# A fused attention and squared-ReLU kernel in which W_out's first blocks are stored earlier, its first further sums stand behind the norms, and the late conversions are placed differently

## The chip, the cores and the metric

The kernel runs on one core of one Trainium2 chip. The metric is device time in microseconds, the median of three runs. The profile is of one further execution with the hardware profiler on.

## What is computed

Linear attention without a softmax, a normalisation per head, and then a two-layer network with a squared ReLU, all in float32:

```python
kv = einsum('bhsd,bhse->bhde', k, v)            # 8 batches, 8 heads, 576 rows, 64 columns
out = einsum('bhsd,bhde->bhse', q, kv)
x = out / sqrt(mean(out * out, axis=-1) + 1e-6) * g_norm
x = x.transpose(0, 2, 1, 3).reshape(4608, 512)
h = x @ w_in                                    # w_in: 512 x 2048
g = maximum(h, 0) ** 2
return g @ w_out                                # w_out: 2048 x 512
```

The two weight matrices arrive as 64-bit floats, which the kernel reads as pairs of 32-bit words and converts itself.

## The kernel before

The 4608 rows are worked through in nine strips of 512 (index `s`). A strip first makes hidden values (the "up" steps), then multiplies them with W_out (the "down" steps). The products use Strassen-like schemes: seven products of blocks take the place of eight, and the sums of blocks that they need are made by VectorE, or by GpSimd, ahead of them. From strip 1 on the down products, and from strip 2 on the up products too, apply the scheme a second time, on 128 by 128 blocks.

Strip 0 is different, because the weights are still being loaded and converted while it runs. Its up steps are sixteen plain steps of `up_first` (4 column groups `g`, 2 halves `fh`, 2 parts `i`), its down steps are seven products `p` in the order 1, 2, 5, 6, 7, 3, 4, each in two halves, by `down`. `n_up` is the number of up steps, 16 here.

All instructions are recorded in program order, and each engine executes its own in that order (the pools are under `tc.manual_schedule()`). So the place of a call in the Python text sets the order of the work on each engine and on SyncE's (SP's) queue, from which nearly all DMAs are issued. In the compiled program the DMA issues take eight completion semaphores in turn, so that an issue also waits for the landing of the DMA eight issues before it.

The parts that matter here:

- `load` and `load_next` bring k, v and q of a batch and a pair of heads. `load_rest(b, eng)` brings the last 64 rows of k and of v for all heads of a batch `b` (`k_rest`, `v_rest`); for batch 0 it is called on ScalarE's queue, after all other first loads. `key_value` multiplies k and v, with the rest rows last, and ScalarE copies the product to `kv_all`.
- `load_piece` brings a raw piece of weights (128 x 512 words of 64 bits, 512 KB) into one of 8 buffers, `load_more` does so some pieces ahead. There are 32 pieces: 0 to 15 of W_in, 16 to 31 of W_out.
- `convert_on_act` makes two passes over a raw piece on ScalarE (`w_c`, and `raw` in place); `conversion` makes four on VectorE (L254 to L263). `convert_pieces` converts a pair of pieces and issues ScalarE's passes for the pair after it. `convert(n)` brings the list `conversions` up to entry `n`: 8 entries of `pieces_in`, 4 of `pieces_out`, 4 of `sums_out`.
- `pieces_out` converts half of W_out into places 4 and 5 of the tile `w_in`, which are free in strip 0. `sums_out` converts the other half into tiles `wt` (in the raw pool), makes the block W_out t1 in place 6 and four further blocks in `wt`, and stores these four in the DRAM tile `w_out`. The three blocks in places 4, 5 and 6 are called `w_first`; strip 0's products 1, 2 and 5 read them there. `down` stores each of them in `w_out` too, in two DMAs of 512 KB, in the step that follows its product. Later `sums_in` (called at down steps 7, 8, 9 and 12) scales W_in by g and overwrites places 4, 5 and 6 with sums of W_in's blocks.
- `deep_sums` makes four further sums of a W_out block on VectorE (`w_t`) and `store_deep_sums` stores them in the DRAM tile `w_deep`. `down` calls it in strip 0, in the first half of each product (in the second half for product 1). `stream` brings the block for a later product back from DRAM into `w_blk`; the tiles `w_t` and `w_blk` share one pool of four buffers, which takes over the memory of the raw pieces.
- `attend(n)` takes the next slices of the attention work: queries transposed (`t_ps`, `qT`), keys and values, products `x_ps`, their squares and means (`sq`, `ms`), roots, the normalised `x_n`, and its transpose `xt_ps` to `xT`. It is called after the products of each step.

The late conversions in strip 0's up steps are placed by these lines of the main loop:

```python
if 4 <= i < 11:
    convert(3 + i)          # ahead of the step's products
...
if 11 <= i < n_up:
    convert(5 + (3 * i + 2) // 4)   # behind the step's attention slices
```

Of the kernel before, what the change touches and what calls it, by code (L numbers as in the profile page):

```python
# [20 lines left out]
def kernel(  # L21
# [34 lines left out]
    nc = tc.nc  # L56
    P = 128
# [91 lines left out]
    def load_rest(b, eng):  # L149
        h = b % 2  # L150
        half = slice(REST * h, REST * (h + 1))
        for t, src in ((k_rest[half], k), (v_rest[half], v)):
            eng.dma_start(out=t, in_=src[b, :, C * P : S].rearrange("h s d -> s h d"))
# [20 lines left out]
    def load_next(q_eng=nc.sync, names="kvq"):  # L174
        u = next(to_load, None)
        if u is not None:
            load(*u, q_eng, names)
# [138 lines left out]
    conversions += [(pieces_out, j) for j in range(0, FQ, 2)] + [(sums_out, j) for j in range(0, FQ, 2)]  # L316
    converted = [NP // 2]

    def convert(n):
        while converted[0] < min(n, len(conversions)):  # L320
            fn, a = conversions[converted[0]]
            fn(a)
            converted[0] += 1
# [9 lines left out]
    nc.scalar.sqrt(one, one)  # L333

    load_next()
    for p in range(1, NP):
        load_next()
        load_piece()
# [2 lines left out]
    g_src = g_norm.rearrange("(d u) -> d u", u=1)  # L341
    for h in range(2):
        nc.scalar.dma_start(out=g_col[ts(h, D)], in_=g_src)
    load_rest(0, nc.scalar)


    qT, kvd, x_n, xt = {}, {}, {}, {}
# [476 lines left out]
    def store_deep_sums(p, w):  # L824
        if p == 6:

            parts = [sum_pool.tile([P, FQ // 2, P], FP32, name=f"w_t{i}", tag="sum") for i in range(4)]
            deep_sums(parts, w)
            for i, t in enumerate(parts):
                nc.sync.dma_start(out=w_deep[B_OUT[p], :, i], in_=t)  # L830
            return
        if p not in deep:
            reserve(p)
        t = deep.pop(p)
        deep_sums([t[:, i] for i in range(4)], w)
        nc.sync.dma_start(out=w_deep[B_OUT[p]], in_=t)

    def down(s, p, i):
        if i == 0:
            open_bank(p)  # L840
        a = {1: 11, 2: 21, 6: 11, 7: 12, 3: 21, 4: 22}.get(p)
        w = w_blk[s, p]
        product(
            p, i,
            lambda fc: (gq[s, 1, fc // 2][:, fc % 2] if p == 5 else gq[s, a][:, fc])[:, ts(i, P)],
            lambda fc: w[:, :, fc], FQ,
        )

        if i == (p == 1) and s == DEEP - 1:
            store_deep_sums(p, w)  # L850
        if i == 0:
            return
        del w_blk[s, p]

        if s == 0 and p in (2, 6, 3):
            reserve({2: 5, 6: 7, 3: 4}[p])
        if p not in (1, 7) and (s, p) not in ((0, 3), (0, 4)):
            stream()
        if s == 0 and p in (1, 2, 5):

            for e in range(2):
                nc.sync.dma_start(out=w_out[B_OUT[p], :, e], in_=w_first[B_OUT[p]][:, :, ts(e, P)])

        if p == (1 if s else 2):
            for g in range(NG):
                x = gq[s, 11][:, ts(g, 2)]
                minus(nc.vector, x, gq[s, 1, g], x)
        if p == (2 if s else 5):
            minus(nc.vector, gq[s, 21], gq[s, 21], gq[s, 11])

        def store(th, eh):
            def f(b, a=None):
                o = out_tile()
                if a is None:
                    nc.scalar.copy(o, b)
                else:
                    nc.vector.tensor_tensor(out=o, in0=b, in1=a, op=ALU.add)
                send(s, th, eh, o)
            return f

        combine(p, store(0, 0), store(0, 1), store(1, 0), store(1, 1))


    deep = {}

    def deep_sums(t, w):
        b11, b12, b21, b22 = (w[:, e, ts(f, FQ // 2)] for f in range(2) for e in (1, 0))
# [278 lines left out]
    for s in range(N_STRIP):  # L1166
        attend(ready[s])
        if s == DEEP_UP - 1:
            while queried:
                attend(slice_at[0] + 1)  # L1170
            psums.close()
            fpsum = ctx.enter_context(tc.tile_pool(name="fpsum", bufs=5, space=bass.MemoryType.PSUM, reuse_waits="tile"))
            apsum = ctx.enter_context(tc.tile_pool(name="apsum", bufs=1, space=bass.MemoryType.PSUM, reuse_waits="tile"))
        if s >= DEEP_UP:
            steps = [(0.5, up_slot, (s, slot)) for slot in range(55)]
        elif s == 0:
            steps = [(2, up_first, (g, fh, i)) for g in range(NG) for fh in range(2) for i in range(2)]
        else:
            steps = [(1, up, (s, g, p)) for g in range(NG) for p in ORDER]
        n_up = len(steps)  # L1180
        if s < DEEP:

            steps += [(2, down, (s, p, i)) for p in (ORDER if s else (1, 2, 5, 6, 7, 3, 4)) for i in range(2)]
        else:
            steps += [(2, down_deep, (s, k, i)) for k in range(7) for i in range(2)]
        goal, begun = ready.get(s + 1, len(slices)), slice_at[0]
        if s >= DEEP_UP:
            goal = max(goal, min(ready[DEEP_UP] + (len(slices) - ready[DEEP_UP]) * (s - 1) // (N_STRIP - DEEP_UP - 1), len(slices)))
        total, done = sum(w for w, _, _ in steps), 0
        for i, (w, fn, a) in enumerate(steps):  # L1190
            if s == 0 and i < n_up:

                if 4 <= i < 11:
                    convert(3 + i)
                if i == 0:
                    load_next()
                    load_rest(1, nc.sync)
                    load_next()
                if i == 1:
                    load_next()  # L1200
                if i == 2:
                    for b in range(2):
                        load_q_rest(b, nc.sync)
            elif s == 0 and i == n_up:
                convert(len(conversions))
                conv.close()

                stream_pool = ctx.enter_context(tc.tile_pool(name="stream", bufs=4, reuse_waits="tile"))
                sum_pool = ctx.enter_context(tc.tile_pool(name="sum", bufs=8, reuse_waits="tile"))
            if s == 0 and n_up <= i < n_up + 2:  # L1210
                for g in range(2 * (i - n_up), 2 * (i - n_up) + 2):
                    sum_g1(0, g)
            if s == 0 and n_up + 2 <= i < n_up + 4:
                for g in range(2 * (i - n_up) - 4, 2 * (i - n_up) - 2):
                    sum_g3(0, g)
            fn(*a)
            if s == 0 and i < 4:

                convert(3 + i)
            done += w  # L1220
            if s:
                clock[0] += 3.2 if i >= n_up else 2.2 if s == DEEP else 1.2
                soon = tiles_due and tiles_due[0][2][0] // NT == s + 1
                if i == n_up + 10:
                    while tiles_due and tiles_due[0][2][0] // NT == s + 1:
                        _, f, a = tiles_due.popleft()
                        f(*a)
                elif not due(keys_due) and not (soon and due(tiles_due)):
                    least = 2.1 if s == DEEP else 4.5 if i < n_up else 3.3
                    if not (n_up * 2 // 3 < i < n_up + 3) and clock[0] >= dripped[0] + least:  # L1230
                        dripped[0] = clock[0]
                        drip(True)
                pace = 25 if s == DEEP else 36
                attend(begun + (goal - begun) * min(i + 1, pace) // pace)
                if s == DEEP and i == n_up - 3:
                    leaf_sums(s, 4)
                if s == 1 and i in range(2, 23, 3):
                    deep_sums_in((1, 6, 5, 4, 0, 2, 3)[i // 3])
                if s == 1 and i in (21, 22, 23, 25):
                    stream()  # L1240
                continue
            if i == n_up + 1:
                stream()
            if i == n_up + 8:
                load_next()
            if i == n_up + 9:
                load_rest(2, nc.sync)
                load_q_rest(2, nc.sync)
            if i - n_up in (7, 8, 9, 12):
                sums_in((7, 8, 9, 12).index(i - n_up))  # L1250
            if i == n_up + 11:
                sums_x(1)
            n = i + 1 - (n_up - 6)
            pairs, m = divmod(max(n - 2 * NP, 0), 3)
            attend(min(ready[0] + min(max(n, 0), 2 * NP) + (n >= 2 * NP) + 4 * pairs + (0, 2, 2)[m], goal))
            if 11 <= i < n_up:

                convert(5 + (3 * i + 2) // 4)


# [28 lines left out]
```

## Time and profile before

| | us |
|---|---|
| median of 3 runs | 914.62 (913.01 to 919.57) |
| profiled execution, device time | 918.22 |
| its span in the profile | 916.2 |
| TensorE busy | 890.1 |
| VectorE busy | 732.8 |
| ScalarE busy | 315.0 |
| GpSimd busy | 306.0 |
| mean DMA rate | 257 GB/s |

The profile is read on several levels: busy time of each engine, busy time in slices, the chain of waits that ended last, and each engine's timeline, in which idle time ahead of an instruction is given with the engine or DMA that ended it. PE is TensorE (PEld its weight loads), DVE VectorE, ACT ScalarE, POOL GpSimd, SP SyncE; SPq and ACTq are issues of DMAs. L754 is line 754 of the kernel before. Who ended a wait is inferred, and where the engine named had long been done, it was another.

### The profile page before, as it was taken

The page shows a single profiled execution, that of the slowest core. Times are in us where ns is not written, and L with a number is a line of the kernel's source. Part 1 is how long each engine was busy: PE and PEld are TensorE (multiplying, and loading weights), DVE is VectorE, ACT ScalarE, POOL GpSimd, SP SyncE. Part 2 cuts the span into 40 slices and gives each one's busy share as a digit, 9 for nine tenths or more (in the row PEclk, how much of TensorE's full clock was granted, in tenths as well). Part 3 has the DMA queues.
Part 4 walks back from the last instruction along what each step waited for, and adds up shares of the span by engine and source line. Part 5 has one row for each costly group of instructions (what it writes and reads, how often), then busy time and mean ns, then how long its engine had stood idle before and what let it go on. Part 6 is the DMA issues. An engine that isn't in the chain of part 4 may idle for free.

```text
span 916.2 us, 20585 instructions
## 1 busy us (share of the span) xinstructions
PE 890.1 (97%) x8246; PEld 828.9 (90%) x8246; DVE 732.8 (80%) x1256; ACT 315.0 (34%) x622; POOL 306.0 (33%) x315
## 2 busy tenths in 40 slices
PE   7898989999999999999999999999999999999998
PEld 6444778889999999999999998999999999999998
DVE  1999787778968895789688967887689868975886
ACT  3797332331023701370128011720263027201710
POOL 0000000830057604560457044514362346234700
PEclk7999999999999999999999999999999999999999
DMA  9896799989989697979877988979656866685385
GB/s 283 263 326 198 226 352 270 275 264 322 311 257 249 223 341 239 264 224 339 267 223 216 330 278 218 262 251 329 207 155 253 310 217 192 251 307 175 123 302 193
DMA packets 172367, 235.71 MB, mean 257 GB/s; under 512 B 83568, under 2 KB 137328, under 8 KB 163824
## 3 DMA queue, kind: packets, MB, share of 16 engines
q1 hardware_dynamic: 171056, 234.14, 80.2%
q8 instruction: 65, 1.06, 0.5%
q10 hardware_dynamic: 1216, 0.26, 0.2%
q14 instruction: 30, 0.25, 0.1%
HBM read 197.66 MB, written 36.70 MB: 256 GB/s over the span
## 4 chain that ended last, share of the span: by engine, by line
PE 76%; DVE 12%; DMA 6%; issue 2%; ACT 2%; SPq 1%; DVEq 0%; ACTq 0%
PE ps_B L928 21%; PE ps_A L928 16%; PE ps_A L1116 16%; PE ps_B L1116 8%; PE ps_C L1116 4%; PE ps_A L708 3%; PE kv_ps L408 3%; PE x_ps L442 2%; PE ps_B L708 1%; DMA w_out<-w_in 1%; DVE w_c L260 1%; DVE w_t L280 1%; DVE gt L1128 1%; DVE ms L459 1%; DMA raw<-in_moe_w_out_dram 1%
## 5 line engine op out<-in xcount | busy, mean ns | idle before, releaser
L928 PE MATMUL ps_B<-w_blk,g_s 128*128 128x128 f32 x1024 | 126.2, 275 | 0.0
L928 PEld LDWEIGHTS ps_B<-w_blk,g_s 128*128 128x128 f32 x1024 | 120.0, 192 | 0.2
L1116 PE MATMUL ps_A<-x_l,w_in 128*128 128x128 f32 x784 | 104.1, 276 | 0.0
L280 POOL TENSOR_TENSOR x_l<-xT 128x256 f32<-128x256 f32 x21 | 15.8, 751 | 244.5 <-PE ps_A L928 244.5
L928 PE MATMUL ps_B<-w_blk,gt 128*128 128x128 f32 x768 | 97.4, 275 | 0.0
L1116 PEld LDWEIGHTS ps_A<-x_l,w_in 128*128 128x128 f32 x784 | 95.4, 192 | 0.5 <-DVE gt L1128 0.2
L928 PE MATMUL ps_A<-w_blk,g_s 128*128 128x128 f32 x768 | 93.6, 275 | 0.0
L928 PEld LDWEIGHTS ps_B<-w_blk,gt 128*128 128x128 f32 x768 | 91.5, 192 | 0.1
L928 PEld LDWEIGHTS ps_A<-w_blk,g_s 128*128 128x128 f32 x768 | 89.6, 192 | 0.0
L1128 POOL TENSOR_TENSOR snap<-snap,gt 128x512 f32<-128x512 f32 x35 | 46.6, 1332 | 123.0 <-ACT snap L1133 65.5
L1133 ACT COPY snap<-ps_A 128x512 f32<-128x512 f32 x63 | 36.7, 582 | 132.7 <-PE ps_A L1116 115.2
L943 DVE TENSOR_TENSOR o_sb<-o_sb,ps_B 128x256 f32<-128x256 f32 (+1 forms) x128 | 49.5, 387 | 34.6 <-ACT o_sb L944 27.3
L1066 ACT ACTIVATE gt<-gt 128x512 f32<-128x512 f32 x112 | 69.7, 622 | 18.3 <-DVE gt L1128 18.2
L928 PE MATMUL ps_A<-w_blk,gt 128*128 128x128 f32 x576 | 72.3, 275 | 1.4 <-DMA w_blk<-w_deep 1.4
L1067 ACT ACTIVATE gt<-gt 128x512 f32<-128x512 f32 x112 | 70.6, 631 | 3.6
L928 PEld LDWEIGHTS ps_A<-w_blk,gt 128*128 128x128 f32 x576 | 68.2, 192 | 1.5 <-DMA w_blk<-w_deep 1.5
L1026 POOL TENSOR_TENSOR w_i<-w_in 128x512 f32<-128x512 f32 x7 | 9.3, 1335 | 160.8 <-DVE w_in L280 160.8
L1128 POOL TENSOR_TENSOR gt<-gt,snap 128x512 f32<-128x512 f32 x42 | 52.5, 1277 | 24.9 <-DVE snap L1128 24.9
L280 DVE TENSOR_TENSOR gt<-gt 128x2048 f32<-128x2048 f32 (+1 forms) x29 | 59.7, 2063 | 0.0
L944 ACT COPY o_sb<-ps_A 128x128 f32<-128x128 f32 x24 | 6.4, 266 | 147.3 <-PE ps_A L928 147.3
L1116 PE MATMUL ps_A<-x_l,w_blk 128*128 128x128 f32 x392 | 52.3, 276 | 1.4 <-issue 1.2
L1116 PE MATMUL ps_B<-x_l,w_blk 128*128 128x128 f32 x392 | 52.0, 276 | 0.0
(176 smaller groups left out, 1822.4 us busy)
## 6 DMA issues: line engine op xcount, KB each, us to landing
w_blk<-w_deep SPq DMA_DIRECT2D x56, 1024.0 KB, 6.8
w_blk<-w_out SPq DMA_DIRECT2D x56, 768.0 KB, 6.0
w_blk<-w_in_deep SPq DMA_DIRECT2D x49, 768.0 KB, 5.0
raw<-in_moe_w_in_dram SPq DMA_DIRECT2D x16, 512.0 KB, 6.1
raw<-in_moe_w_out_dram SPq DMA_DIRECT2D x16, 512.0 KB, 5.9
k<-in_k_dram SPq DMA_DIRECT2D x29, 256.0 KB, 4.7
v<-in_v_dram SPq DMA_DIRECT2D x29, 256.0 KB, 5.1
x_d<-x_q SPq DMA_DIRECT2D x27, 256.0 KB, 5.5
```

The costliest lines, as they stand in the source:

```text
L280: eng.tensor_tensor(out=out, in0=a, in1=b, op=ALU.subtract)
L408: nc.tensor.matmul(ps[ts(h, D), i], lhsT=a, rhs=w, start=c == 0, stop=c == C)
L442: nc.tensor.matmul(ps[half, r, i, ts(p, D)], lhsT=q[row, half], rhs=kvd[b, p][row, row], start=True, stop=True)
L708: nc.tensor.matmul(bank[BANK[p]][:, i, :], lhsT=lhsT(k), rhs=rhs(k), start=p in (1, 5, 2) and i == 0 and k == 0, stop=k == n - 1, skip_gro ...
L928: nc.tensor.matmul(chain[c][x][:, i, :], lhsT=a[:, f, :], rhs=w[:, f, :], start=x not in opened[c] and f == 0, stop=f == FQ // 2 - 1, skip ...
L943: add = lambda out, a, b: nc.vector.tensor_tensor(out=out, in0=a, in1=b, op=ALU.add)
L1026: nc.gpsimd.tensor_tensor(out=s1, in0=w_half(b, 0, 1), in1=w_half(b, 1, 1), op=ALU.add)
L1066: nc.scalar.activation(o, o, AF.Relu)
L1067: nc.scalar.activation(o, o, AF.Square)
L1116: nc.tensor.matmul(ps[:, i, :], lhsT=w, rhs=rhs, start=j in (1, 2, 5) and i == 0, stop=True, skip_group_check=True)
L1128: add = lambda eng, out, a, b: eng.tensor_tensor(out=out, in0=a, in1=b, op=ALU.add)
L1133: nc.scalar.copy(t, ps)
```

## The change

1. `load_rest(0)` is called right after the first pair's loads, and on SyncE's queue instead of ScalarE's.
2. The stores of the three blocks `w_first` leave `down`. A new function `store_first(b)` issues them: block 0 ahead of the products of up step 12, block 1 ahead of up step 13, block 2 at the first down step, after the last conversion.
3. `down` no longer calls `store_deep_sums` itself, but puts the block in a queue `deep_due`, which is emptied at the end of each step, after the attention slices, except in the second down step. So the further sums of product 1 are made a step later, together with those of product 2, and all of them behind the slices of their step.
4. The conversion that stood ahead of up step 10 is made behind up step 11, and the last three move from behind steps 12, 13 and 14 to behind 13, 14 and 15.

No arithmetic is added or removed. The number of DMAs and their sizes stay the same.

```diff
+    def store_first(b):
+        for e in range(2):
+            nc.sync.dma_start(out=w_out[b, :, e], in_=w_first[b][:, :, ts(e, P)])
+
@@ first loads
     load_next()
+    load_rest(0, nc.sync)
     for p in range(1, NP):
         load_next()
         load_piece()
...
-    load_rest(0, nc.scalar)
@@ down
         if i == (p == 1) and s == DEEP - 1:
-            store_deep_sums(p, w)
+            deep_due.append((p, w))
...
-        if s == 0 and p in (1, 2, 5):
-
-            for e in range(2):
-                nc.sync.dma_start(out=w_out[B_OUT[p], :, e], in_=w_first[B_OUT[p]][:, :, ts(e, P)])
-
...
-    deep = {}
+    deep, deep_due = {}, deque()
@@ main loop
-                if 4 <= i < 11:
+                if 4 <= i < 10:
                     convert(3 + i)
...
+                if i in (12, 13):
+                    store_first(i - 12)
             elif s == 0 and i == n_up:
                 convert(len(conversions))
                 conv.close()
+                store_first(2)
...
             attend(min(ready[0] + min(max(n, 0), 2 * NP) + (n >= 2 * NP) + 4 * pairs + (0, 2, 2)[m], goal))
+            while deep_due and i != n_up + 1:
+                store_deep_sums(*deep_due.popleft())
             if 11 <= i < n_up:
-                convert(5 + (3 * i + 2) // 4)
+                convert((13, 13, 14, 15, 16)[i - 11])
```

## The prediction

> **What bounds the kernel now.** I read the page's busy shares, then the chain of waits, then the timeline of each engine from 0 to 175 us, which is all that the change touches. In these fences a row is start, duration, engine, line, operation, tiles, shape, and in brackets the idle time ahead of it with what ended it.
>
> ```profile
> PE 890.1 (97%) x8246; PEld 828.9 (90%) x8246; DVE 732.8 (80%) x1256; ACT 315.0 (34%) x622; POOL 306.0 (33%) x315
> PE 76%; DVE 12%; DMA 6%; issue 2%; ACT 2%; SPq 1%; DVEq 0%; ACTq 0%
> ```
>
> TensorE bounds the whole: 890.1 of 916.2 us. At most 26.1 us can be won without removing matmuls. The idle rows of TensorE say where they lie:
>
> ```profile
> 10.52 0.43 PE L408 MATMUL kv_ps<-v_rest,k_rest 64*64 64x64 f32 x4 [1.81 <-DMA v_rest<-in_v_dram]
> 78.89 1.11 PE L384 MATMUL t_ps<-ident,q 128*128 128x128 f32 x4 [2.54 <-ACT qT L386]
> 98.52 0.66 PE L384 MATMUL t_ps<-ident,q 128*128 128x128 f32 x4 [0.97 <-ACT qT L386]
> 118.63 1.32 PE L570 MATMUL xt_ps<-ident,x_n 128*128 128x128 f32 x8 [3.13 <-DVE x_n L510]
> 149.31 7.17 PE L708 MATMUL ps_A<-w_blk,gt 128*128 128x256 f32 x32 [1.27 <-DVE o_sb L877]
> 173.86 0.63 PE L570 MATMUL xt_ps<-ident,x_n 128*128 128x128 f32 x4 [0.79 <-DVE x_n L510]
> ```
>
> These are 10.5 us. Up to 40 us the chain passes through loads, TensorE and VectorE; from 52 to 75 us it is VectorE's conversions (L254 to L263) without a gap; from 149 us it is TensorE. So in 40 to 130 us the clock of the kernel is VectorE, and the waits of TensorE at 78.89 and 98.52 only bring forward what 118.63 would cost anyway. VectorE's own gaps are then the price list:
>
> ```profile
> 96.13 0.43 DVE L254 TENSOR_SCALAR w_c<-w_c 128x512 f32<-128x512 f32 x1 [0.94 <-ACT w_c L242]
> 109.24 0.69 DVE L280 TENSOR_TENSOR w_t<-w_in 128x512 f32<-128x512 f32 x1 [4.52 <-DMA w_out<-wt]
> 117.88 1.29 DVE L510 TENSOR_TENSOR x_n<-x_ps,newton 128x512 f32<-128x512 f32 x2
> 130.78 1.29 DVE L510 TENSOR_TENSOR x_n<-x_ps,newton 128x512 f32<-128x512 f32 x2
> 142.17 1.29 DVE L280 TENSOR_TENSOR w_in<-w_in 128x512 f32<-128x512 f32 x2 [4.91 <-DMA w_out<-w_in]
> ```
>
> The reader is to see that the first x_n stands behind the 4.52, and that the 4.91 is a store out of W_in's places which the next sums overwrite. ScalarE and the chain show the late raw pieces:
>
> ```profile
> 74.76 0.69 ACT L242 ACTIVATE w_c<-raw 128x512 f32<-128x512 f32 x1 [0.17 <-DVE w_in L263]
> 78.25 0.59 ACT L386 COPY qT<-t_ps 128x512 f32<-128x512 f32 x1
> 94.04 0.69 ACT L242 ACTIVATE w_c<-raw 128x512 f32<-128x512 f32 x1 [7.79 <-DVE wt L280]
> 86.83 8.52 DMA raw<-in_moe_w_out_dram
> 131.44 10.61 DMA w_out<-w_in
> ```
>
> The last raw piece was issued at 86.83 and landed at 95.35, just before the second w_c at 95.43: that wait is the load's, not VectorE's.
>
> **What the Trainium skill says.** "DMA: Bandwidth & Descriptors", section "Issuing engines are not separate DMA queues": a transfer moved from ScalarE's queue to SyncE's runs on the same engines and only the issue time changes. The trace agrees as far as it goes: v_rest took 5.33 us from ScalarE's queue, SyncE's neighbours of the same size 5.2 and 5.6. Same page, "Anatomy of one DMA": waits are on the issuing sequencer, so one waiting issue holds all behind it; the trace has SyncE's loads held so at 81 to 98 us. "TensorE: Matmul & The Clock Gate", Part 1: after about 3.4 us of idleness TensorE runs at half clock for such a window. Here the windows are seen after shorter waits already, 2.54 and 3.13 us:
>
> ```profile
> 78.90:82.30 3.40, 3.40 (x7) 1.91 (x8) 3.40 (x11) 3.30 (x10) 0.00 (x0) 0.50 0.23 89
> 119.85:123.25 3.40, 3.40 (x10) 2.69 (x10) 3.40 (x6) 0.65 (x2) 0.00 (x0) 0.50 1.02 319
> ```
>
> The last but two column is the clock. The second made 16 matmuls of L708 take 5.31 us where their sisters took 3.62: about 1.7 us a window.
>
> **The change part by part**, in the profiled execution's time.
>
> *The first rest rows on SyncE.* k_rest and v_rest are issued fifth and sixth on SyncE, at about 3.3 and 3.9 us, where the two q loads of the next pair stood, which landed at 8.56 and 9.51. These shared the engines with k_rest from ScalarE's queue, which now isn't beside them, so I take 8.9 for v_rest instead of 10.48. TensorE's wait shrinks by 1.6. The two issues cost SyncE 1.3 us, inside its hold of 4.54 to 6.33 us. The next pair's v landed at 11.71 and was used at 14.46, so it carries the shift. From 11 to 40 us TensorE, ScalarE and VectorE follow one another, so the 1.6 reaches VectorE's conversions. Bounds: 0.5, if v_rest is as late as the sixth transfer was; 4, if the shorter wait also spares the half clock that the trace has from 10.6 to 20.85 us (9.3 us of TensorE on the chain, of which loads and VectorE would give back half). I take 1.6.
>
> *Late conversions spread.* In the listing of the program's order the pairs of ScalarE passes over raw 26/27, 28/29 and 30/31 (four passes, 2.3 us each pair) stand behind more of the ReLUs and copies. The first goes behind the qT copy of 78.25, which then ends near 76.3: TensorE's 2.54, its half clock window of 1.2 (L749 4.84 for 3.60) and, by the next pair, 0.97 go. VectorE needs raw 26/27 at 81.7 and gets them at 80.3. So 4.7 us on TensorE, but off the chain: worth nothing by itself, and it covers what follows.
>
> *Stores as soon as converted, a cost ahead.* Four stores of 512 KB now stand on SyncE between the first four wt stores (VectorE ends their data at 81.7) and the loads k, v, four q, raw 30, raw 31. In the listing the issues take eight semaphores in turn, each waits for the landing of the one eight before: raw 30 waits for the third store, raw 31 for the fourth. Stores of this size landed 1.45 to 2.6 us apart, mean 1.8; the wt stores, 0.7 apart, end at 85.8. So the fourth lands at 85.8 + 4 x 1.8 = 93.0, raw 31 is issued then, and with the 4.9 us of an unhindered raw load (63.56) it lands at 97.9, against 95.35. Behind it wait raw 31's w_c, then VectorE's L254, and on ScalarE the last ReLU and kv_all's copy, for which TensorE waits at its fourth kv product (97.3 to about 101). VectorE loses 2.6 more than the 0.94 it loses now. Bounds: 1.2 (stores 1.45 apart) and 5.8 (2.6 apart).
>
> *First further sums behind the norms.* The eight w_t sums (8 x 0.61) go behind x_n. By then the wt stores have landed, so the 4.52 goes whole; nothing is added to VectorE. VectorE is ahead by 4.52 - 2.6 = 1.9 at the second x_n: its first half ends at 131.4 - 1.9 = 129.5. TensorE, which passed there at 133.12 unhindered but 1.7 us behind the data, would be there at 126.7 and now waits: 3.6 won. That wait of 2.8 us may bring the half clock as the 2.54 did: 1.7, and I take half, 0.8.
>
> *The stores again.* VectorE's 4.91 goes, as the last of the six stores is issued near 107 and landed by 114, while sums_in comes after 132. W_out's streamed block for product 6 is issued after the last wt store has landed (about 110), lands near 118, wanted at 119.7. TensorE's 1.27 at 149.31 goes, and with VectorE further ahead the 0.79 at 173.86.
>
> Sum: 1.6 + 3.6 - 0.8 + 1.3 + 0.8 = 6.5 us. The profiled execution, 918.22 us (2.0 around its span), would become 911.7; it stands 3.6 above the median 914.62, and the same gain from the median gives 908.1. From 215 us on nothing is moved: the listing shows TensorE's order unchanged throughout.
>
> **Rivals.**
> *All of it counts:* the opening keeps full clock (2.4 more), no half clock at the second x_n (0.8), stores at 1.45 us (4 x 0.35 = 1.4 less stall): 11.1 us, 903.5. For it: a measurable part of the loss now is clock. Against: TensorE is still idle over 1 us in the window that decides.
> *Hidden anyway:* the stores run 2.6 apart beside the loads, the stall is 5.8, VectorE is 1.3 later than now at the second x_n but TensorE had 1.7 in hand there, so 0.4 stays of the 3.6: 1.6 + 0.4 + 1.3 + 0.8 less a half clock window of 1.7 is 2.4, 912.2. For it: 2.6 was measured with other transfers beside.
> *The other side:* the last raw pieces behind 2 MB of stores become the bound. Each us that raw 31 lands beyond 104.4 (97.9 + 6.5) is lost whole, for VectorE, ScalarE and TensorE all stand behind it. At 4.5 us a store it lands at 108.7: 4.3 slower, 919. For it: one queue, eight in flight. Against: 1 MB blocks took 2.5 to 3.9, so this is over twice the worst store.
>
> **How the numbers follow.** Forecast 0.50, all counts 0.25, hidden 0.17, the other side 0.08. 1% is 9.1 us, about what a measurement of this kernel tells from no change. Faster by over 1%: the second case and a tenth of the forecast, 0.30. Slower by over 1% needs half of the last case and unseen mishaps, 0.07. Within: 0.63. The range takes in 13.6 us won to 1.4 us lost (unknown costs at their ends): 901 to 916.
>
> **What would show it.** Right: kv_ps's wait for v_rest under 0.5 us; no wait at the second L384; raw's last load landing 2 to 4 us later against VectorE's conversions, with a longer L254 gap and a new TensorE wait at kv_ps near 96 to 100; no gap before w_t; none at w_in L280 for w_out; TensorE's wait for x_n moved to the second L570. Wrong: if raw 31 is no later than now, the store step is wrong and the gain is over 9; if VectorE's gap there is above 6, the gain is gone; if the rest rows land after 10, the first step is.

## The result, and the profile after

| | time before | time after | after / before | 95% interval |
|---|---|---|---|---|
| 22 runs of each | 915.76 us median | 913.81 us median | 0.9974 | 0.9960 to 0.9987 |
| 14 runs after, 48 before, another chip | 916.24 us | 913.98 us | 0.9965 | 0.9950 to 0.9981 |

The change wins about 2 to 3 us. The prediction said 6.5. The sign and the range hold, the size doesn't: less than half of what was forecast came. The profiled execution took 915.83 us (before 918.22). The page of the changed kernel (busy shares, then the shares of the chain that ended last):

```profile
span 913.7 us, 20581 instructions
PE 887.0 (97%) x8246; PEld 827.8 (91%) x8246; DVE 734.1 (80%) x1256; ACT 315.0 (34%) x622; POOL 306.4 (34%) x315
PE 81%; DVE 9%; DMA 5%; SPq 2%; issue 2%; POOL 1%; ACT 1%; DVEq 0%; ACTq 0%
```

TensorE is idle for 26.7 us still (913.7 - 887.0, and 26.1 before): its busy time fell by 3.1 us, its idle time did not fall at all. So the 26.1 us of idle time were no ceiling for a gain, as the prediction has it: matmuls slowed by half clock count as busy. On the chain TensorE has 81% in place of 76%, VectorE 9% in place of 12%: VectorE's stretch is shorter, but not gone.

TensorE's idle rows, to be laid beside those of before (start, duration, engine, line, tiles, and in brackets the idle time ahead):

```profile
8.51 0.47 PE L412 MATMUL kv_ps<-v_rest,k_rest 64*64 64x64 f32 x4 [0.93 <-DMA v_rest<-in_v_dram]
103.64 1.12 PE L412 MATMUL kv_ps<-v,k 128*64 128x64 f32 x16 [8.20 <-ACT kv_all L416]
132.45 1.22 PE L574 MATMUL xt_ps<-ident,x_n 128*128 128x128 f32 x8 [1.70 <-DVE x_n L514]
171.48 0.63 PE L574 MATMUL xt_ps<-ident,x_n 128*128 128x128 f32 x4 [0.50 <-DVE x_n L514]
```

The waits of 2.54, 0.97, 3.13 and 1.27 us are gone, as predicted. In their place stands one of 8.20 us, for which the prediction had about 3.7. VectorE's timeline says where it comes from:

```profile
100.12 0.43 DVE L254 TENSOR_SCALAR w_c<-w_c 128x512 f32<-128x512 f32 x1 [7.53 <-ACT w_c L242]
101.58 0.43 DVE L254 TENSOR_SCALAR w_c<-w_c 128x512 f32<-128x512 f32 x1 [1.04 <-ACT w_c L242]
113.66 1.29 DVE L514 TENSOR_TENSOR x_n<-x_ps,newton 128x512 f32<-128x512 f32 x2
131.61 1.29 DVE L514 TENSOR_TENSOR x_n<-x_ps,newton 128x512 f32<-128x512 f32 x2
```

VectorE now idles 7.53 + 1.04 = 8.57 us ahead of the last conversion, where it idled 0.94. The gaps of 4.52 (w_t) and 4.91 (w_in) are gone, but the second x_n, which decides, comes at 131.61, later than the 130.78 of before. The chain of waits names the cause (SPq is SyncE's sequencer issuing):

```profile
87.92 1.49 SPq L130
94.76 6.04 DMA raw<-in_moe_w_out_dram
100.89 0.67 ACT w_c L242
101.58 0.43 DVE w_c L254
```

Raw 31, the last piece, is issued at 94.76 and lands at 100.80. Before, it landed at 95.35. The table by stretch has, ahead of the last two columns (DMA share and GB/s), the granted clock:

```profile
103.60:107.00 3.40, 3.36 (x85) 3.13 (x86) 3.40 (x9) 1.54 (x5) 0.00 (x0) 0.50 0.80 238
82.00:101.00 19.00, 13.44 (x71) 9.23 (x69) 11.02 (x28) 5.15 (x11) 0.00 (x0) 0.99 1.05 270
```

From 82 to 101 us the DMA engines are full at 270 GB/s, which suggests that the piece waited for bytes; the experiments below test it. After the 8.20 us wait TensorE runs at half clock (0.50).

### The profile page after: what moved, and what is told of

It reads as the page before. It is cut to its first block, busy times and chain, and to the rows that moved or that the text cites. A ratio compares the mean times of both kernels' runs of the same rounds, so it can differ in the third digit from the quotient of the medians.

```text
span 913.7 us, 20581 instructions
## 1 busy us (share of the span) xinstructions
PE 887.0 (97%) x8246; PEld 827.8 (91%) x8246; DVE 734.1 (80%) x1256; ACT 315.0 (34%) x622; POOL 306.4 (34%) x315
## 4 chain that ended last, share of the span: by engine, by line
PE 81%; DVE 9%; DMA 5%; SPq 2%; issue 2%; POOL 1%; ACT 1%; DVEq 0%; ACTq 0%
PE ps_B L927 20%; PE ps_A L1115 16%; PE ps_A L927 15%; PE ps_B L1115 8%; PE ps_A L712 4%; PE ps_C L1115 4%; PE kv_ps L412 2%; PE ps_A L753 2%; PE ps_B L712 2%; DMA w_blk<-w_deep 2%; PE ps_C L753 2%; PE x_ps L446 1%; PE ps_B L753 1%; DVE o_sb L942 1%; DVE gt L1127 1%
## 5 line engine op out<-in xcount | busy, mean ns | idle before, releaser
L927 PE MATMUL ps_B<-w_blk,gt 128*128 128x128 f32 x768 | 97.5, 275 | 0.1
```

Of the source, the lines that this page charges most:

```text
L927: nc.tensor.matmul(chain[c][x][:, i, :], lhsT=a[:, f, :], rhs=w[:, f, :], start=x not in opened[c] and f == 0, stop=f == FQ // 2 - 1, skip ...
```

## The experiments

All ratios are to the kernel before on the same chip. "Lead" is how much earlier the same matmul starts than in the profile of before; I take it at matmul record 1200, counted from 0 (200.36 us in before), and at record 1600 (253.94). A lead comes from one profiled execution and can lie some us off the typical one: the late conversions alone lead by 3.8 us at 200 us and by -0.2 at the end, and their time is that of before.

### The opening alone

```diff
# the kernel before
     load_next()
+    load_rest(0, nc.sync)
     for p in range(1, NP):
...
-    load_rest(0, nc.scalar)
```

> The kernel before with one part of the change alone: k_rest and v_rest issued fifth and sixth on SyncE. Theory (the opening's gain is carried through): the first kv product's wait falls from 1.81 to about 0.9 us, all of 11 to 175 us lies 2.0 us earlier, and the time falls by 2.0 us, that is most of the 1.95 us that the whole change brought, so the other parts cancel to nothing. Rival (it is swallowed later, as the loads and stores of 80 to 110 us set VectorE's end): the opening is 2.0 earlier, but x_n L510 at 117.88 and 130.78 is not, and the time is within 0.5 us of before.

Measured: 913.65 us, 0.9962 (0.9948 to 0.9977), some 3.5 us won, more than expected and no less than the whole change. So the rest of the change together added nothing that can be measured. The profile is that kernel's slowest execution (917.04, median 913.65), and its lead of 4.0 us at 200 us is down to 1.3 past 254: a loss far behind the change, taken up below.

The opening's own size is seen better over all profiles made for this study. Matmul record 200 starts at 44.63, 42.16 and 42.34 us in three executions with the old opening (mean 43.0), and at 40.0 to 42.9 in eleven with the new (mean 41.5): 1.5 us. Much of the spread is clock. In the profile of before TensorE ran at half clock for 10.2 us of the opening, in the two others with the same opening for 3.4. The rows are before's and that of a version with the same opening (before with the queries later, below); the last but two column is the mean clock:

```profile
10.60:20.85 10.25, 9.05 (x64) 7.93 (x66) 3.77 (x11) 4.44 (x12) 0.00 (x0) 0.50 1.11 378
10.60:20.85 10.25, 8.18 (x78) 7.06 (x79) 4.61 (x16) 5.29 (x14) 0.00 (x0) 0.83 1.10 378
```

Among the profiles with 10.2 us of half clock the new opening is 2.1 us earlier at record 200 (three profiles against one), among those with 3.4 us it is 1.4 earlier (five against two). So the profile of before was a slow draw, by some 2 us, and a lead over it is read most fairly from a profile with as much half clock in its opening. The profile of the changed kernel is one: it has 10.2 us too.

### The late conversions alone

```diff
# the kernel before
-                if 4 <= i < 11:
+                if 4 <= i < 10:
                     convert(3 + i)
...
-                convert(5 + (3 * i + 2) // 4)
+                convert((13, 13, 14, 15, 16)[i - 11])
```

> The kernel before with the late conversions' spreading alone. ScalarE's passes over raw 26 to 31 move behind ReLUs and copies, and on SyncE raw 28/29 move behind the loads of one pair, raw 30/31 behind those of the next, as in the changed kernel; no stores ahead of them. Theory bytes: raw 31 lands near 97.5, 2 us later than the 95.35 of before, VectorE's w_t still waits for the wt stores, the second x_n is 2 us later and TensorE has 1.7 in hand there, so the time is within 1 us of before. Theory order: raw 31 lands at 99.5 or later, TensorE waits at kv_ps for 6 us or more and the kernel is 2.5 to 4 us slower than before.

Measured: 915.81 us, 1.0003 (0.9984 to 1.0022): nothing, as the theory of bytes had it. Raw 31 landed at 93.05, earlier than the 97.5 of that theory and earlier than in the kernel before, whose profile runs 2.5 us behind this one at record 200. So its new place, behind the loads of one more pair, is not what makes it late. TensorE's and VectorE's rows:

```profile
113.66 1.97 PE L570 MATMUL xt_ps<-ident,x_n 128*128 128x128 f32 x8 [4.80 <-DVE x_n L510]
104.27 0.69 DVE L280 TENSOR_TENSOR w_t<-w_in 128x512 f32<-128x512 f32 x1 [1.84 <-DMA w_out<-wt]
```

The waits of 2.54 and 0.97 us have moved into the wait for x_n, 4.80 for 3.13: TensorE arrives earlier at the data that decides.

### The stores behind the raw loads, and half of them ahead

```diff
# the changed kernel
-                if i in (12, 13):
-                    store_first(i - 12)
+                if i in (14, 15):
+                    store_first(i - 14)
```

> The changed kernel, with the four stores of W_out's first two blocks issued two steps later, behind the loads of raw 30 and 31; the order on TensorE, VectorE, ScalarE and GpSimd is the same. Theory bytes (the last raw loads were late because 2 MB of stores drain ahead of them): raw 31 lands near 93.5 in place of 100.81, VectorE's two gaps of 7.53 and 1.04 at L254 shrink to 1.5 together, TensorE's wait of 8.20 at kv_ps goes, the second x_n comes 7 us earlier, and the kernel is 7 us faster than the changed one, 907 us. Theory order (they were late because the change put them behind k and v of the third batch, and k's issue waits for TensorE's third kv product at 87.6): raw 31 lands after 98.5 and at most 2.5 us are won. Both together: raw loads issued near 90.7, landed near 95.5, some 5 us won.

```diff
# the changed kernel: same four stores ahead, half the bytes in each
-    def store_first(b):
+    def store_first(b, js=slice(0, FQ)):
         for e in range(2):
-            nc.sync.dma_start(out=w_out[b, :, e], in_=w_first[b][:, :, ts(e, P)])
+            nc.sync.dma_start(out=w_out[b, :, e, js], in_=w_first[b][:, js, ts(e, P)])
...
-                    store_first(i - 12)
+                    store_first(i - 12, slice(0, FQ // 2))
...
                 store_first(2)
+                for b in range(2):
+                    store_first(b, slice(FQ // 2, FQ))
```

> The changed kernel with the same four stores, but only the first half of each (256 KB) ahead of the raw loads; the other halves are issued behind the last of the six stores. As many issues stand ahead of the raw loads as in the changed kernel, with half the bytes. Theory bytes: raw 31 lands half as late, near 97.0, and about 3.8 us are won against the changed kernel. Theory issues (eight in flight, each issue waits for the one eight before): the same count, so raw 31 within 1 us of 100.8. Theory order (k's wait for TensorE's product): within 1.5 us of 100.8 too.

These two with the last one and the two kernels show why raw 31 is late. From the traces' transfers, counted from the landing of the first wt store so that a different opening cancels:

| kernel | stores ahead of raw 31 | first wt store | raw 31 | between |
|---|---|---|---|---|
| before | none | 83.66 | 95.35 | 11.69 |
| late conversions alone | none | 81.87 | 93.05 | 11.18 |
| stores behind | none | 82.08 | 93.23 | 11.15 |
| half stores | 4 x 256 KB | 80.21 | 95.03 | 14.82 |
| changed | 4 x 512 KB | 82.51 | 100.80 | 18.29 |

The delay is 0, 3.6 and 7.1 us for 0, 1024 and 2048 KB: 3.6 us for each 1024 KB, which is 290 GB/s. (Half stores also have half as many packets, so bytes and packets are not told apart here.) "Eight in flight" is not it. The equal count of issues in the last two rows does not show that by itself, as half stores also land sooner, but the changed kernel's trace does: the fourth store, eight issues ahead of raw 31, landed at 93.17, and raw 31 was issued 1.6 us later; the seven issues before it came 3 to 6 us after the landings that they could have waited for. Nor is it k's wait for TensorE's product, which the chain of the changed kernel shows at 87.92: with the stores behind, k is issued at 82.22, ahead of that product. The chain named the last event before a late issue; what made the issue late was the full queue. SyncE's issues from the stores to raw 31 took up to 1.8 us each there, against 0.4 to 0.6 at 70 to 74 us, and these transfers landed in the order of their issue. This agrees with the Trainium skill, "DMA: Bandwidth & Descriptors", section "Queues, rings and completion order": each DMA engine consumes the descriptors of a queue in order, so bytes issued ahead are served ahead. VectorE's waits with none and with half:

```profile
94.03 0.43 DVE L254 TENSOR_SCALAR w_c<-w_c 128x512 f32<-128x512 f32 x1 [1.21 <-ACT w_c L242]
```

```profile
94.12 0.43 DVE L254 TENSOR_SCALAR w_c<-w_c 128x512 f32<-128x512 f32 x1 [2.92 <-ACT w_c L242]
95.80 0.43 DVE L254 TENSOR_SCALAR w_c<-w_c 128x512 f32<-128x512 f32 x1 [1.25 <-ACT w_c L242]
```

The times moved less than the theory of bytes had it: stores behind 911.92 us, 0.9949 (0.9931 to 0.9967), where 907 was expected; half stores 914.02 us, 0.9973 (0.9956 to 0.9990), no better than the changed kernel, where 3.8 us were expected. The idle rows of TensorE with the stores behind show what took the gain's place:

```profile
96.11 0.69 PE L412 MATMUL kv_ps<-v,k 128*64 128x64 f32 x16 [1.04 <-ACT kv_all L416]
116.60 8.83 PE L712 MATMUL ps_A<-w_blk,gt 128*128 128x256 f32 x32 [2.14 <-DMA w_blk<-w_out]
128.29 1.94 PE L574 MATMUL xt_ps<-ident,x_n 128*128 128x128 f32 x8 [2.86 <-DVE x_n L514]
247.27 1.85 PE L927 MATMUL ps_A<-w_blk,gt 128*128 128x128 f32 x8 [2.49 <-DMA w_blk<-w_deep]
```

The 8.20 is down to 1.04. But the 2048 KB still have to go out: now the block for product 6 is late (2.14, with a half clock window, 8.83 us for 7.17), and VectorE's w_t wait 3.29 us for a w_deep store. The second x_n comes at 127.4, 4.2 earlier instead of 7. The lead at 200 us is 5.58; at 254 us 2.04 are left, the rest having gone in waits of 0.52 and 2.49 us for W_out's streamed blocks and in the half clock after.

### The sums back ahead of the norms

```diff
# the version with the stores behind
-            deep_due.append((p, w))
+            store_deep_sums(p, w)
```

> The kernel of the stores behind raw 30 and 31, with the further sums w_t put back ahead of the norms, as in the kernel before. Theory (the sums behind the norms are worth their 4.52 us of wait once the raw loads are in time): VectorE waits 5 us or more ahead of w_t near 102, the second x_n moves from 127.4 to 131 or later, and TensorE's lead at 200 us falls from 5.6 to 2 us; with the floor at 248 us the end is 1 to 2 us later than without this edit. Rival (the sums cost nothing where they stood): lead at 200 us within 1 us of 5.6, the same time.

```profile
108.38 0.69 DVE L280 TENSOR_TENSOR w_t<-w_in 128x512 f32<-128x512 f32 x1 [5.15 <-DMA w_out<-wt]
117.77 1.97 PE L574 MATMUL xt_ps<-ident,x_n 128*128 128x128 f32 x8 [8.13 <-DVE x_n L514]
```

The wait is back, 5.15 us, the second x_n comes at 129.9 for 127.4 (131 or later was expected), and the lead at 200 us is 3.04 for 5.58: the mechanism is as predicted, somewhat smaller. Past 254 us nothing of it is left in these two profiles, 3.36 for 2.04. The time is 912.83 us, 0.9963 (0.9950 to 0.9976), in the expected direction, but its interval overlaps that of the version without this edit.

### The queries behind the blocks

In 205 to 250 us of the kernel before, the table by stretch has the DMA engines 97% busy at 318 GB/s:

```profile
205.00:250.00 45.00, 44.57 (x354) 43.11 (x352) 41.11 (x67) 4.43 (x11) 0.29 (x1) 1.00 0.97 318
```

Small q loads stand between the blocks there. The next edit puts them behind:

```diff
# four kernels: stores behind (twice), before, changed
-                    if not (n_up * 2 // 3 < i < n_up + 3) and clock[0] >= dripped[0] + least:
+                    if not (n_up * 2 // 3 < i < n_up + (10 if s == DEEP else 3)) and clock[0] >= dripped[0] + least:
```

> The kernel of the stores behind raw 30 and 31, and one more edit: the small loads of q and q_rest (32-row tiles, twelve of them between 228 and 244 us) that stand between the streamed W_out blocks of strip 1 are issued after these blocks; only SyncE's order changes. Theory floor (in 205 to 250 us the DMA engines are full, so the block w_deep wanted near 244 lands at a time that does not follow TensorE's lead, and what exceeds some 3.7 us of lead is lost there[...]): the wait of 2.49 us at 247 falls below 1.4, no half clock follows, TensorE keeps 4.5 or more of its 5.6 us of lead past 255 us, and the time falls another 2.5 us, to some 909 us. Rival (the bytes of the blocks themselves are the limit, or the late queries stall strip 2): within 0.5 us of the kernel without this edit.

> The kernel before with the same postponement of the small q loads in strip 1, and nothing else. Theory floor: its own wait of 1.36 us at 250.93 goes, 1.0 to 1.4 us are won. Rival (late queries stall strip 2, or nothing changes): within 0.5 us of before, or slower.

> The changed kernel with the small q and q_rest loads of strip 1 behind that strip's W_out blocks, and nothing else. Theory floor: the changed kernel's two profiles lead before by 2.7 and 4.1 us at 200 us, but keep 2.3 and 0.4 of it past 254 us; here the waits for w_deep between 240 and 249 us are below 0.5 us in all, the lead past 254 us is 4 us or more, and the time is 0.9955 of before, 1 us or more under the changed kernel. Rival (the lead is lost elsewhere, the changed kernel's medians already hold what can be had): 0.997 of before.

> The version with the stores behind raw 30 and 31 and the queries later once more, on the chip of the other three: 0.993 of before; lead past 254 us of 5 us or more.

> The changed kernel once more, on the chip of the three others. Expected: 0.997 of before, TensorE's lead 2.4 us at 175 us and at the end; the version with the stores behind the raw loads 0.002 to 0.003 below it if the late raw loads are what cost it, equal if the floor at 248 us takes back everything.

| kernel | lead at 200 | lead past 254 | half clock in the opening | same three with queries later | time with queries later |
|---|---|---|---|---|---|
| before | 0 | 0 | 10.2 us | 2.40, 4.02, 3.4 us | 0.9993 (0.9977 to 1.0010) |
| changed | 2.70 | 2.33 | 10.2 us | 2.85, 4.47, 6.8 us | 0.9978 (0.9963 to 0.9994) |
| changed, again | 4.06 | 0.36 | 3.4 us | | |
| stores behind | 5.58 | 2.04 | 10.2 us | 6.05, 7.67, 3.4 us | 0.9931 (0.9908 to 0.9955) |
| stores behind, again | | | | 5.38, 7.00, 10.2 us | 0.9931 (0.9911 to 0.9951) |

With the queries later TensorE waits nowhere in 205 to 250 us, and every lead grows by 1.62 us there, close to the wait of 1.36 us that before's own profile has at 250.93. Without, leads of 4.0 (opening alone), 4.1 and 5.6 us shrink there to 1.3, 0.4 and 2.0, while leads of 2.7 to 3.8 us in the four other profiles are kept to within 0.4. The second profile of the changed kernel shows how, waits and then half clock (24 such matmuls took 2.84 us elsewhere):

```profile
240.15 1.16 PE L927 MATMUL ps_B<-w_blk,gt 128*128 128x128 f32 x8 [0.89 <-DMA w_blk<-w_deep]
248.94 1.79 PE L927 MATMUL ps_A<-w_blk,gt 128*128 128x128 f32 x8 [2.20 <-DMA w_blk<-w_deep]
250.53 3.66 PE L927 MATMUL ps_A<-w_blk,g_s 128*128 128x128 f32 x22
```

The times say less. On before and on the changed kernel the edit won nothing that can be measured, where 1.0 to 1.4 us and a ratio of 0.9955 were expected. The three profiles with the half clock at 248 us (opening alone 917.04, stores behind 916.20, changed again 918.23) are each the slowest of their kernel's 18, 11 and 14 runs. That suggests that the typical execution loses less there, but doesn't show it: 13 of the 14 profiled executions of this study are slower than their kernel's median, with that half clock or without. On the stores behind the edit gave 910.49 and 909.30 us, the lowest ratio of the study, twice; its intervals overlap those of the version without, 0.9949. The lead lost at 248 us is thus shown for some executions; what it costs the median stays open.

One comparison here is clear in time. On one chip, with the queries later in both, the changed kernel ran 914.02 us (22 runs) and the stores behind 909.30 (6 runs); their intervals, 0.9963 to 0.9994 and 0.9911 to 0.9951, do not meet. The two differ only in the place of the four stores. So with the queries later that place costs some 4.7 us (3.1 between the two profiled executions), about what the change fell short of its forecast. Without the queries later the difference is smaller and the intervals overlap.

### The stores later still

```diff
# stores behind, queries later: the last four (then all six) stores
-                if i in (14, 15):
-                    store_first(i - 14)
+                if i == 15:              # absent in the second version
+                    store_first(0)
...
-                store_first(2)
...
             while deep_due and i != n_up + 1:
                 store_deep_sums(*deep_due.popleft())
+            if i == n_up + 2:
+                store_first(1)           # second version: 0, 1 and 2
+                store_first(2)
```

> The version with the stores behind raw 30 and 31 and the queries later, and the last four of the six stores moved once more: behind the streamed block for product 6 and the first two w_deep stores. Theory (each 512 KB store delays whatever SyncE issues after it by some 1.8 us): the block lands near 110, TensorE's wait of 1.98 us for it at 114 and its half clock go; VectorE's wait of 3.64 us at 118 for a w_deep store goes; the second x_n comes 3.5 us earlier and TensorE's lead at 160 us grows from 5.3 to 8 us or more; 2.5 us faster than without this edit, 908 us. Rival (the stores now hold up W_in's further sums at 132 us, or the block for product 7): VectorE waits 4 us or more for w_out<-w_in as in the kernel before, and nothing is won.

> The same with all six stores behind the block for product 6. Theory: the wt stores land 3.6 us earlier still, but the last of the six stores lands near 127 to 130, next to the further sums of W_in at 130: as the last experiment or up to 1 us faster, and slower than it by 1 to 3 us if VectorE waits for a store there.

First TensorE's rows with four stores later, then with all six:

```profile
122.37 1.23 PE L574 MATMUL xt_ps<-ident,x_n 128*128 128x128 f32 x8 [3.03 <-DVE x_n L514]
126.08 9.86 PE L712 MATMUL ps_A<-w_blk,gt 128*128 128x256 f32 x32 [2.49 <-DMA w_blk<-w_out]
```

```profile
131.24 9.22 PE L712 MATMUL ps_A<-w_blk,gt 128*128 128x256 f32 x32 [6.05 <-DMA w_blk<-w_out]
```

The waits for product 6's block and for w_t go, as expected, but product 7's block, issued behind the stores, is late: 2.49 us after four of them, 6.05 after six. W_in's sums don't wait. Times: 910.10 us, 0.9943 (0.9922 to 0.9964), and 914.71 us, 0.9981 (0.9970 to 0.9993). Each place that was tried makes another transfer late. The four stores later bring nothing measurable over the version they start from, where 908 us was expected and a lead of 8 us at 160 us (it was 6.7), though their one profile has the largest lead of the study past 254 us, 9.1. Six lose most of what that version had won.

The lowest ratio has the version with the stores behind raw 30 and 31 and the queries later: 0.9931 both times, 910.49 us where the changed kernel ran 913.98 on the same chip. It beats before clearly. Its intervals end at 0.9955 and 0.9951, and those of the changed kernel begin at 0.9960 and 0.9950.

## Why the prediction was wrong, point by point

*The rest rows on SyncE (1.6 us).* About right: 1.5 over fourteen profiles, 1.4 and 2.1 where the half clock is the same. v_rest landed at 8.37, where I took 8.9. The wait shrank only to 0.93, not below 0.5, because the first v too came 1.1 us earlier. That the change spares half clock there, as its bound of 4 allows, is not shown: the half clock varies from execution to execution, with 10.2 us in the first profiles of both kernels and 3.4 us in others of both openings. In the time the part alone won some 3.5 us (2.1 to 4.8 by its interval); why more than 1.5 is not settled.

*Late conversions (4.7 us off the chain, worth nothing).* Right: TensorE gained 5.2 us between the opening and 100 us (lead 7.2 at matmul record 400 against 2.0 at 200), and alone the part measured 1.0003.

*The stores' cost ahead (2.6 us).* This is the step that failed. The sum was made in before's time; the changed kernel is there 2.0 us further on, so 2.0 is added to its times here. "The wt stores, 0.7 apart, end at 85.8" was 87.5: 1.7 more (the trace of before has 86.6 already, as they are not all 0.7 apart). "4 x 1.8" for the stores was 7.7, 0.5 more. And "with the 4.9 us of an unhindered raw load" was 7.6 us (93.17 to 100.80), 2.7 more: the load was not unhindered. k, v and four q parts (768 KB; 2.9 us at 270 GB/s) and raw 30 were queued behind the same stores, ahead of raw 31, and the text listed them but did not price them. Together 4.9 us: VectorE idles 8.57 - 0.94 = 7.6 more, not 2.6.

The prediction's own sign, a gap above 6 and the gain is gone, came; what stayed of the time is no more than the opening alone wins. The 7.6 is beyond the 5.8 of the rival "hidden anyway". A gain like its 2.4 us came, and as it said the stall eats the sums' gain. But it had the stores land 2.6 us apart, and they were 1.9 apart on the mean, so the closeness of the number is in part luck. Nothing tied the upper bound to the bytes in the queue. All 3840 KB from the end of the wt stores (85.48) to raw 31, at the 270 GB/s of this trace, give 14.6 us, and the trace has 15.3. The same sum for the half stores (2816 KB) gives 10.7 for 10.9 us, and for the stores behind (1792 KB) 6.8 for 8.2.

*The sums behind the norms (4.52 whole).* Right: no gap ahead of w_t, and 5.15 us of it when put back.

*The second x_n (3.6 won, 0.8 lost to clock).* Follows the failed step: first half ready at 132.31 + 2.0 = 134.3, not 129.5, so TensorE lost 1.3 there instead of winning 3.6. No half clock followed the wait of 1.70; it followed the 8.20 instead.

*1.27 and 0.79.* The first went, the second shrank to 0.50. The sum is then 2.0 - 1.3 + 1.3 + 0.3 = 2.3 us; the lead at 182 us in the trace is 2.4, and 2.5 at the end. This sum explains one profile against another. It does not prove the size of the gain, as before's order with less half clock in the opening leads by 2.1 us at the same place without any of the change (the profile with the queries later); for the size the medians stand, 2 to 3 us apart.

*"From 215 us on nothing is moved."* True of the order, but read as if a gain would pass through. The runs show a stage with the DMA engines full, where three profiles with leads of 4.0 to 5.6 us kept only 0.4 to 2.0 of them. The chance of 0.25 for 11.1 us had no answer to that.

## What to carry to other kernels

When transfers are moved ahead of a load, price the load's landing as all bytes queued ahead of it, over the rate the full queue shows, not as its usual latency plus the moved transfers; small loads in between count. A gain must also get through every later stage that is already full: look for the next wait on a transfer behind the change and at the DMA share there. And compare one profiled execution with the median of the runs before its idle times are taken as a price list: the opening of before was slow by 2 us in the profile that I read, for its half clock.

## What the runs showed of the hardware

*The clock.* Half clock comes in stretches of 3.4 us or of a multiple of it (but for the one at each trace's end), and in each of the 14 traces every such stretch begins a whole number of steps of 3.41 us after the first one. Divide each trace from 20 us on, without its last four steps, by this measure: in 24 of the 3573 steps at full clock TensorE was idle for 1.95 us or more, and after 23 of them the next step ran at half clock; after the 3549 others none did. So it is not the length of a wait that counts in these traces, but the idle time within one step. Waits of 2.14, 2.20 and 2.49 us, each within one step, were followed by half clock (8.83 us for 7.17; 1.79 and 1.85 for 1.16). A wait of 2.50 us in before with the queries later (ahead of 76.56) lay across two steps, 1.4 and 1.1 us, and had none. After the wait of 3.03 us above the transposes still ran at full clock (1.23 us), and the half clock came at the next step, at 124.8. In the opening half clock also followed less idle time, 1.6 us in one step; why is open.

*The DMA queue.* SyncE's queue moved 270 GB/s at 82 to 101 us, with stores and loads of 256 to 512 KB and q loads of 64 KB in it, and 318 GB/s at 205 to 250 us, mostly with blocks of 768 and 1024 KB. In the first stretch a load landed after all that had been issued ahead of it.
